# Four places for the values, other places for the results, and side work in other slots, in a fused attention and gated MLP kernel

## The chip, the cores and the metric

The kernel runs on one core of a Trainium2 chip. The core has five engines with their own instruction queues: TensorE (PE in the rows, with PEld for its weight loads), VectorE (DVE), ScalarE (ACT), GpSimd (POOL) and SyncE (SP, which here only issues DMAs). Each engine works through its own list in order and waits on semaphores. The metric is the device time of one execution in microseconds; before the change it was 2021.7 us, the median of three runs (2020.38 to 2023.5).

## The reference, cut to what matters

Four sequences of 3008 tokens go through an attention without softmax, and all 12032 tokens then go through a gated MLP. Everything is float32.

```python
scores = (z @ z.T) / S                  # per batch, z is S x 64
attn = np.maximum(scores, 0.0) ** 2
x = u * (attn @ v)                      # u, v: 4 x 3008 x 256
gate = 1 / (1 + np.exp(-(x @ w_gate)))  # 256 -> 1536
val = x @ w_val
out = (gate * val) @ w_out              # 1536 -> 256
```

## The kernel before, in words

**Float32 from two halves.** Operands of matmuls are split in a rounded high part and a low rest (`x_high` and `x_low`, `h_high` and `h_low`, and so on), and a product is three matmuls: high by high, high by low, low by high.

**Stage 1, attention.** `steps` is a list of 288 steps: 4 batches of 72, in each of them 6 chunks of 512 queries, in each of these 12 pairs of key blocks. In a step PE computes scores two steps ahead and then the product with v. ACT takes scale, relu and square and rounds the result (`ah`, line 367); DVE takes the rest (`al`, line 372). Scores are symmetric, so later chunks load stored, turned blocks back (`r<-shared`, line 461) in place of computing them. Work that isn't part of a step is hung on step numbers in the tables `before` and `after`: loads of the next batch, the eighteen `Narrow` jobs that turn the weights from float64 words into halves and store them in DRAM (line 726 ff.), and, in the last twelve steps, the making of the first group's x. The attention's sums go to the DRAM tensor `sums`.

**Stage 2, the MLP.** Tokens go in 12 groups of 1024 (two tiles t of 512; the last group 2 of 384), and a group takes six rounds J, one for each 256 columns of the hidden width. In a round the 2 x 2 blocks of x by weights are made with seven products in place of eight (Winograd's form of Strassen's scheme), once for the gate and once for the value: P1, P6, P2, P7, P5, P4, P3, each three matmuls into one of PSUM's banks 0 to 3, which are taken in turn. `copy_s1` (ACT) and seven `join`s (DVE, line 641) add the products up to four blocks, named 11, 21, 12 and 22. Gate blocks lie in `g_t` (four places in the area `spare`), value blocks in `y_t` (area `keep`). `gate` is ACT's sigmoid, `gated` (POOL, line 649) multiplies value by gate, `h_high` (ACT, line 653) and `h_low` (POOL, line 658) split the result. Its product with `w_out`, eight outs of three matmuls (lines 674 to 676), runs one round later: after the second, fourth, fifth and last product of gate and of value, `beside` puts one out. So the order on PE in a round is, for the gate and again for the value: P1 P6 out P2 P7 out P5 out P4 P3 out, 66 matmuls in all.

**Slots.** `beside(J, slot)` also runs what the table `extra` holds for that slot; slots 0 to 3 lie in the gate's half, 4 to 7 in the value's. Slots 0 and 4 stand after the join of P6, 1 and 5 after that of P7, 2 and 6 after those of P5, 3 and 7 after the last join of the half, that of P3. On DVE such side work stands between these joins. It is what the next group needs: `load_sums`, `load_u` (8 DMAs of 64 KB for one tile t), `turn_u` (a transpose of u), `make_x` (u times sums), `sum_x` (T1 to T4, four differences), and four times `x_high` and `x_low`. `finish` transposes a finished result out of PSUM and sends it out with four DMAs.

**What sets the order.** The order is written by hand; nothing is scheduled anew. An instruction waits until its inputs are there and until earlier readers of the place that it writes are done. Before the change the four value blocks share two places: 11 and 21 have one, 22 and 12 the other. A join that writes 12 thus waits for the `gated` that reads 22.

The places that the change touches, for following it in the code:

```python
t = part(keep_a, 4 * (C % 2), 2 * CH)                      # line 504, keep
y_t = {c: part(keep_a, 2 * x, CH) for c, x in ((11, 0), (22, 1), (21, 0), (12, 1))}   # line 625
osb = t_p[:, 2 + h] if t else part(keep_a, 4 + 2 * h, CH)  # line 681, finish
```

## Time and profile before

| what | value |
|---|---|
| median of three runs | 2021.7 us |
| the profiled execution | 2018.66 us |
| its span in the trace | 2016.2 us |
| PE busy | 1918.4 us, 95% |
| DVE busy | 1505.0 us, 75% |
| ACT busy | 1151.9 us, 57% |
| POOL busy | 781.3 us, 39% |
| granted TensorE clock | 0.999 of full speed (2.4 GHz) |

The page cuts the span in 40 slices. PE stands at 9 tenths or more in all of them but two, at 8. POOL is at three tenths in the first slice, at zero up to the eighteenth and at five to seven tenths in the rest: stage 2 begins at about 895 us. A matmul's record is longer than the step from one matmul to the next, since matmuls are pipelined; PE's progress is read from starts, and its losses from the waits that the trace puts down to another engine. The profiled execution is 3.0 us under the median of the runs.

### The profile page before, as it was taken

To read this page: it belongs to the slowest core of one execution; us is meant where nothing else is said; L and a number is where in the kernel's file an instruction comes from. 1 tells how busy PE (TensorE), PEld (TensorE's weight loads), DVE (VectorE), ACT (ScalarE), POOL (GpSimd) and SP (SyncE) were. 2 spreads that over 40 slices of the span, in tenths; PEclk is the share of its full clock that TensorE was granted. 3 is DMA by queue.
4 is the path that set the end of the run, shared out by engine and by line. 5 is a ranking of instruction groups with operands and counts; after the bars stand their busy time and mean duration, and the time that the engine had idled before them with its cause. 6 is when DMAs were issued, how large, how long until landed. Compare 5 with 4: busy or idle time off the path is not lost.

```text
span 2016.2 us, 26100 instructions
## 1 busy us (share of the span) xinstructions
PE 1918.4 (95%) x8870; PEld 1649.7 (82%) x8870; DVE 1505.0 (75%) x1946; ACT 1151.9 (57%) x1504; POOL 781.3 (39%) x609
## 2 busy tenths in 40 slices
PE   9999999999999999999989999999999999999998
PEld 7887988798887988887878777777777777778787
DVE  7688788787887776567776867676767777777765
ACT  8886888768886787644434434343434343434443
POOL 3000000000000000007766767676767666767675
PEclk9999999999999999999999999999999999999999
DMA  6689689996899797776324251414152423333231
GB/s 139 142 236 255 193 197 240 259 287 153 227 267 248 219 237 184 195 187 213 92 81 108 66 120 71 118 55 118 56 132 70 107 86 87 93 98 80 83 95 34
DMA packets 596725, 298.76 MB, mean 148 GB/s; under 512 B 529904, under 2 KB 547056, under 8 KB 596592
## 3 DMA queue, kind: packets, MB, share of 16 engines
q1 hardware_dynamic: 591312, 294.48, 55.4%
q0 software_dynamic: 1024, 2.10, 0.5%
q8 instruction: 69, 1.13, 0.2%
q10 hardware_dynamic: 4256, 0.52, 0.2%
q14 instruction: 64, 0.52, 0.1%
HBM read 189.92 MB, written 101.06 MB: 144 GB/s over the span
## 4 chain that ended last, share of the span: by engine, by line
PE 40%; POOL 27%; issue 18%; SPq 4%; ACT 4%; DVE 3%; DMA 3%; DVEq 0%; POOLq 0%; ACTq 0%
POOL spare L649 13%; PE banks L494 9%; PE banks L487 9%; PE banks L489 8%; POOL h L658 8%; POOL v L658 4%; PE banks L344 3%; PE banks L343 3%; POOL al L658 2%; PE banks L616 2%; ACT h L653 2%; PE banks L618 2%; PE banks L617 2%; DMA r<-shared 1%; PE banks L675 1%
## 5 line engine op out<-in xcount | busy, mean ns | idle before, releaser
L649 POOL TENSOR_TENSOR spare<-keep,spare 128x512 f32<-128x512 f32 (+1 forms) x284 | 360.3, 1279 | 1139.6 <-DMA turned<-in_u_dram 854.3
L372 DVE TENSOR_TENSOR al<-r,ah 128x1024 fp32r<-128x1024 f32 (+1 forms) x287 | 341.3, 1191 | 179.0 <-ACT ah L367 173.9
L487 PE MATMUL banks<-ah,v 128*128 128x512 f32 (+1 forms) x1152 | 429.6, 376 | 5.2 <-ACT ah L367 4.8
L489 PE MATMUL banks<-ah,v 128*128 128x512 f32 (+1 forms) x1104 | 414.2, 375 | 0.0
L494 PE MATMUL banks<-al,v 128*128 128x512 f32 (+1 forms) x1152 | 341.1, 378 | 10.9 <-DVE al L372 9.5
L367 ACT ACTIVATE ah<-r 128x1024 fp32r<-128x1024 f32 (+1 forms) x251 | 255.4, 1034 | 51.6 <-DMA r<-shared 15.6
L645 ACT ACTIVATE spare<-spare 128x512 f32<-128x512 f32 (+1 forms) x288 | 177.8, 619 | 166.4 <-DVE spare L641 166.2
L494 PEld LDWEIGHTS banks<-al,v 128*128 128x128 f32 x1152 | 215.6, 189 | 46.2 <-DVE al L372 21.3
L487 PEld LDWEIGHTS banks<-ah,v 128*128 128x128 f32 x1152 | 218.3, 189 | 34.3 <-ACT ah L367 8.1
L653 ACT ACTIVATE h<-spare 128x512 fp32r<-128x512 f32 (+1 forms) x144 | 89.6, 622 | 271.0 <-POOL spare L649 268.6
L658 POOL TENSOR_TENSOR h<-spare,h 128x512 fp32r<-128x512 f32 (+1 forms) x144 | 213.1, 1480 | 55.9 <-ACT h L653 55.9
L641 DVE TENSOR_TENSOR zt<-banks,zt 128x512 f32<-128x512 f32 (+1 forms) x288 | 193.2, 671 | 52.8 <-ACT zt L635 45.4
L489 PEld LDWEIGHTS banks<-ah,v 128*128 128x128 f32 x1104 | 209.2, 189 | 24.4
L351 ACT ACTIVATE r<-banks 128x1024 f32<-128x1024 f32 (+2 forms) x173 | 167.2, 967 | 99.3 <-PE banks L344 97.6
L641 DVE TENSOR_TENSOR spare<-banks,zt 128x512 f32<-128x512 f32 (+1 forms) x288 | 187.0, 669 | 31.9 <-POOL v L658 21.8
L641 DVE TENSOR_TENSOR keep<-banks,zt 128x512 f32<-128x512 f32 (+1 forms) x144 | 97.1, 674 | 117.6 <-POOL spare L649 111.8
L352 ACT ACTIVATE r<-r 128x1024 f32<-128x1024 f32 (+2 forms) x173 | 174.3, 1008 | 5.5
L616 PE MATMUL banks<-z,v 128*128 128x512 f32 x378 | 146.9, 389 | 21.2 <-DVE keep L641 9.8
L653 ACT ACTIVATE v<-spare 128x512 fp32r<-128x512 f32 (+1 forms) x144 | 89.4, 621 | 117.5 <-POOL spare L649 114.8
L618 PE MATMUL banks<-z,v 128*128 128x512 f32 x378 | 143.3, 379 | 0.0
L635 ACT ACTIVATE zt<-banks 128x512 f32<-128x512 f32 (+1 forms) x144 | 83.2, 577 | 91.1 <-PE banks L618 77.6
L343 PE MATMUL banks<-zq,z 128*128 128x512 f32 (+2 forms) x348 | 126.7, 367 | 1.4 <-DVE zq L775 1.4
(150 smaller groups left out, 3828.8 us busy)
## 6 DMA issues: line engine op xcount, KB each, us to landing
v<-w_gv SPq DMA_DIRECT2D x75, 896.0 KB, 4.7
r<-shared SPq DMA_DIRECT2D x72, 512.0 KB, 4.7
shared<-turned SPq DMA_DIRECT2D x236, 128.0 KB, 2.9
r<-shared SPq DMA_DIRECT2D x38, 448.0 KB, 5.0
shared<-spare SPq DMA_DIRECT2D x128, 128.0 KB, 3.3
turned<-sums SPq DMA_DIRECT2D x22, 512.0 KB, 5.9
turned<-in_u_dram SPq DMA_DIRECT2D x176, 64.0 KB, 2.5
w_gv<-w SPq DMA_DIRECT2D x24, 448.0 KB, 4.2
```

Of the source, the lines that this page charges most:

```text
L343: nc.tensor.matmul(sc[:, j, 0 : n - q0], h, q, start=True, stop=False)
L367: nc.scalar.activation(ah[:, :, 0:n], r[:, :, 0:n], AF.Copy)
L372: nc.vector.tensor_tensor(al[:, :, 0:n], r[:, :, 0:n], f32(ah[:, :, 0:n]), op=ALU.subtract)
L487: nc.tensor.matmul(o, vh[:, j, ds], moving(ah[:, j, 0:n]), start=(k == 0 and j == 0), stop=False)
L489: nc.tensor.matmul(o, vl[:, j, ds], moving(ah[:, j, 0:n]), start=False, stop=False)
L494: nc.tensor.matmul(acc[:, d, 0:n], vh[:, j, ds], moving(al[:, j, 0:n]), start=False, stop=stop)
L616: nc.tensor.matmul(o, wt[:, 0, w], xh, start=True, stop=False)
L618: nc.tensor.matmul(o, wt[:, 1, w], xh, start=False, stop=True)
L641: nc.vector.tensor_tensor(to[:, 0:m], bank(J, value, name), s_t[other][:, 0:m], op=ALU.add)
L649: (nc.vector if J == last else nc.gpsimd).tensor_tensor(g, y, g, op=ALU.mult)
L653: nc.scalar.activation(h_of(c)[0][:, 0:m], g_t[c][:, 0:m], AF.Copy)
L658: nc.gpsimd.tensor_tensor(lo[:, 0:m], g_t[c][:, 0:m], f32(hi[:, 0:m]), op=ALU.subtract)
```

## The change

It does these things:

- `y_t` has four places, in all of `keep_a`. `gated` writes its product into the value's place and not the gate's, and `h_high` and `h_low` read it there; the gate's place is free once `gated` has run.
- `finish` puts all four results in the area of x's sums `t_p` (the upper half of `turned_a`), none in `keep_a`.
- `load_u` for the first tile of the next group moves from slot 0 of the group's first round to slot 3 of the second, behind the DMAs of `finish` on SP's queue; `turn_u`, `make_x`, `sum_x`, `x_high`, `x_low` of the next group get other slots.
- The first group's sums, u and x are loaded, turned and multiplied at steps 226 to 247 (early in the last batch) and not in the last twelve, in areas that are free there (`raw_a`, `zt_a`, half of `keep_a`); the sums and splits of it stay in the last twelve steps.
- The eighteen `Narrow` jobs start at other steps: two and not five in the first batch, seven in the second and the third, two early in the last. Three of the five weight loads of the last batch are put later.

```diff
@@ keep
-        t = part(keep_a, 4 * (C % 2), 2 * CH).rearrange("p (h q) -> p h q", h=NB)
+        if C == B * NCH - 1:
+            t = part(turned_a, 8, 2 * CH)
+        else:
+            t = part(keep_a, 4 * (C % 2) if b < B - 1 else 0, 2 * CH)
+        t = t.rearrange("p (h q) -> p h q", h=NB)
...
+    def x_of(G):
+
+        return part(turned_a if G else raw_a, 0, 8 * KB).rearrange("p (t h q) -> p t h q", t=2, h=NB)
+
+    def u_of(G):
+
+        places = (t_p[:, 0:2], t_p[:, 2:4]) if G else (part(zt_a, 0, 2 * CH), part(keep_a, 4, 2 * CH))
+        return places if G else [ap.rearrange("p (i q) -> p i q", i=2) for ap in places]
...
-    y_t = {c: part(keep_a, 2 * x, CH) for c, x in ((11, 0), (22, 1), (21, 0), (12, 1))}
+    y_t = {c: part(keep_a, 2 * x, CH) for x, c in enumerate((11, 21, 12, 22))}
...
-        (nc.vector if J == last else nc.gpsimd).tensor_tensor(g, y, g, op=ALU.mult)
+        (nc.vector if J == last else nc.gpsimd).tensor_tensor(y, y, g, op=ALU.mult)
...
-        nc.scalar.activation(h_of(c)[0][:, 0:m], g_t[c][:, 0:m], AF.Copy)
+        nc.scalar.activation(h_of(c)[0][:, 0:m], y_t[c][:, 0:m], AF.Copy)
...
-        nc.gpsimd.tensor_tensor(lo[:, 0:m], g_t[c][:, 0:m], f32(hi[:, 0:m]), op=ALU.subtract)
+        nc.gpsimd.tensor_tensor(lo[:, 0:m], y_t[c][:, 0:m], f32(hi[:, 0:m]), op=ALU.subtract)
...
-        osb = t_p[:, 2 + h] if t else part(keep_a, 4 + 2 * h, CH)
+        osb = t_p[:, 2 * t + h]
...
-        starts = [*range(24, 54, 7), *range(84, 127, 7), *range(156, 199, 7)][: 3 * NF]
+        starts = [24, 31, *range(84, 127, 7), *range(156, 199, 7), 221, 228]
...
+        g = 3 * per
+        at(after, g + 2, load_w, 0, 1)
+        at(after, g + 6, load_w, 1, 1)
+        for t in range(2):
+            at(after, g + 10 + t, load_sums, 0, t)
+        for t in range(2):
+            at(after, g + 14 + 10 * t, load_u, 0, t)
+            at(before, g + 20 + 10 * t, turn_u, 0, t)
+            at(before, g + 21 + 10 * t, make_x, 0, t)
+        for J in range(3):
+            at(after, g + 28 + 5 * J, load_w, J, 0)
...
-                at(extra, (J, 0), load_u, G, 0)
-                    (1, 3, turn_u, 0), (1, 3, load_u, 1), (1, 6, make_x, 0), (2, 3, turn_u, 1), (2, 6, make_x, 1),
+                    (1, 3, load_u, 0), (1, 7, turn_u, 0), (1, 7, load_u, 1), (2, 3, make_x, 0), (2, 7, turn_u, 1),
...
```

On DVE, in the second round of a group (L641 is the join before, L652 the same line in the change; `banks` are PSUM, `zt`, `spare` and `keep` hold partial sums, gate blocks and value blocks; L552 and L565 are `turn_u`). Before:

```order
L641 TENSOR_TENSOR spare<-banks,spare 128x512
L641 TENSOR_TENSOR spare<-banks,zt 128x512
L552 STREAM_TRANSPOSE turned<-turned 128x1024
L641 TENSOR_TENSOR zt<-banks,zt 128x512
L641 TENSOR_TENSOR keep<-banks,zt 128x512
```

In the change:

```order
L652 TENSOR_TENSOR spare<-banks,spare 128x512
L652 TENSOR_TENSOR spare<-banks,zt 128x512
L652 TENSOR_TENSOR zt<-banks,zt 128x512
L652 TENSOR_TENSOR keep<-banks,zt 128x512
L652 TENSOR_TENSOR spare<-banks,zt 128x512
L652 TENSOR_TENSOR keep<-banks,spare 128x512
L652 TENSOR_TENSOR zt<-banks,zt 128x512
L652 TENSOR_TENSOR keep<-banks,spare 128x512
L652 TENSOR_TENSOR keep<-banks,zt 128x512
L565 STREAM_TRANSPOSE turned<-turned 128x1024
L652 TENSOR_TENSOR zt<-banks,zt 128x512
```

The transpose of u stood after the gate's last join; it stands seven joins later, after the value's last join.

On SP, from the sums' load of one group to the next weight loads (L544 and L556 are `load_u`, L685 and L696 the DMAs of `finish`, L593 and L604 `load_w`). Before:

```order
L533 DMA turned<-sums 128x2x512 x2
L544 DMA turned<-in_u_dram 32x16x32 x8
L685 DMA out_dram<-keep 32x16x32 x8
L685 DMA out_dram<-turned 32x16x32 x4
L593 DMA v<-w_gv 128x1792
L685 DMA out_dram<-turned 32x16x32 x4
L544 DMA turned<-in_u_dram 32x16x32 x8
L593 DMA v<-w_gv 128x1792 x5
```

In the change:

```order
L545 DMA turned<-sums 128x2x512 x2
L696 DMA out_dram<-turned 32x16x32 x12
L604 DMA v<-w_gv 128x1792
L696 DMA out_dram<-turned 32x16x32 x4
L556 DMA turned<-in_u_dram 32x16x32 x16
L604 DMA v<-w_gv 128x1792 x5
```

The first eight loads of u moved from ahead of the sixteen result DMAs to behind them.

On DVE, in the fourth to sixth round of a group (L581 and L592 are `x_low`, L572 and L583 `sum_x`, here of an odd to even group, whose operands lie in `z` and `zq`). Before:

```order
L572 TENSOR_TENSOR turned<-turned 128x512
L641 TENSOR_TENSOR spare<-banks,zt 128x512 x2
L641 TENSOR_TENSOR spare<-banks,spare 128x512
L641 TENSOR_TENSOR zt<-banks,zt 128x512
L572 TENSOR_TENSOR turned<-turned 128x512
L641 TENSOR_TENSOR spare<-banks,spare 128x512
L641 TENSOR_TENSOR spare<-banks,zt 128x512
L581 TENSOR_TENSOR z<-turned,z 128x1024
L641 TENSOR_TENSOR zt<-banks,zt 128x512
L572 TENSOR_TENSOR turned<-turned 128x512
L641 TENSOR_TENSOR keep<-banks,zt 128x512
```

In the change:

```order
L592 TENSOR_TENSOR z<-turned,z 128x1024
L652 TENSOR_TENSOR zt<-banks,zt 128x512
L583 TENSOR_TENSOR turned<-turned 128x512
L652 TENSOR_TENSOR spare<-banks,zt 128x512 x2
L583 TENSOR_TENSOR turned<-turned 128x512
L652 TENSOR_TENSOR spare<-banks,spare 128x512
L652 TENSOR_TENSOR zt<-banks,zt 128x512
L652 TENSOR_TENSOR spare<-banks,spare 128x512
L652 TENSOR_TENSOR spare<-banks,zt 128x512
L583 TENSOR_TENSOR turned<-turned 128x512
L652 TENSOR_TENSOR zt<-banks,zt 128x512
```

The first split now stands ahead of the differences, at the end of a round's value half, and the differences go in slots 0, 1, 3 and 4.

## Rows read from the trace of the kernel before

**Rows 1.** Waits from 905 to 1920: engine, line, releaser: us, times, longest.
```profile
DVE keep L641 <- POOL spare L649: 100.9, 61, 1.8
DVE turned L552 <- DMA out_dram<-turned: 38.3, 9, 5.3
PE banks L616 <- DVE keep L641: 23.5, 42, 0.6
PE banks L675 <- POOL h L658: 19.9, 32, 1.1
...
PE banks L616 <- DVE zt L641: 16.8, 10, 2.8
...
PE banks L616 <- DVE spare L641: 5.3, 20, 0.3
...
PE banks L675 <- POOL al L658: 3.0, 10, 0.3
```
**Rows 2.** PE, same place in two following groups: start, us, line, [idle before, releaser].
```profile
1204.21 0.48 PE L616 MATMUL banks<-x,v 128*128 128x512 f32 x1 [1.49 <-DVE zt L641]
...
1299.24 0.48 PE L616 MATMUL banks<-z,v 128*128 128x512 f32 x1 [1.54 <-DVE zt L641]
```
**Rows 3.** PE, the value's P1 in two following rounds that have no wait.
```profile
1358.88 0.38 PE L616 MATMUL banks<-z,v 128*128 128x512 f32 x1
1373.13 0.38 PE L616 MATMUL banks<-v 128*128 128x512 f32 x1
```
**Rows 4.** Timeline of all engines at the end of such a round.
```profile
1366.01 0.38 PE L616 MATMUL banks<-v,wgv 128*128 128x512 f32 x1
...
1366.19 2.53 POOL L649 TENSOR_TENSOR spare<-keep,spare 128x512 f32<-128x512 f32 x2
...
1366.90 0.60 ACT L635 ACTIVATE zt<-banks 128x512 f32<-128x512 f32 x1 [2.02 <-PE banks L618]
...
1367.51 0.69 DVE L641 TENSOR_TENSOR keep<-banks,zt 128x512 f32<-128x512 f32 x1 [1.83 <-POOL spare L649]
```
**Rows 5.** DVE in a group's second round: the transpose of u.
```profile
1297.36 1.25 DVE L552 STREAM_TRANSPOSE turned<-turned 128x1024 f32<-128x1024 f32 x1 [3.98 <-DMA out_dram<-turned]
```
**Rows 6.** SP's queue: the last result DMAs of that group change.
```profile
1290.40 2.20 SPq L685 DMA_DIRECT2D out_dram<-turned  x4
```
**Rows 7.** SP's queue: the second eight loads of u in the first group.
```profile
918.18 11.78 SPq L544 DMA_DIRECT2D turned<-in_u_dram  x8
```
**Rows 8.** DMA issues: KB each, median us from issue to landing.
```profile
turned<-in_u_dram SPq DMA_DIRECT2D x176, 64.0 KB, 2.5
```
**Rows 9.** Timeline, side work of DVE beside POOL: `make_x`, then `sum_x`.
```profile
1301.69 1.22 DVE L562 TENSOR_TENSOR turned<-turned 128x1024 f32<-128x1024 f32 x1
1301.88 2.15 POOL L658 TENSOR_TENSOR h<-spare,h 128x512 fp32r<-128x512 f32 x1 [0.74 <-ACT h L653]
...
1321.39 1.28 POOL L658 TENSOR_TENSOR al<-spare,v 128x512 fp32r<-128x512 f32 x1
...
1321.66 1.55 DVE L572 TENSOR_TENSOR turned<-turned 128x512 f32<-128x512 f32 x1
1322.62 1.74 POOL L649 TENSOR_TENSOR spare<-keep,spare 128x512 f32<-128x512 f32 x1
```
**Rows 10.** End of stage 1: DVE's transpose of u for the first group.
```profile
882.64 1.25 DVE L552 STREAM_TRANSPOSE turned<-turned 128x1024 f32<-128x1024 f32 x1 [4.60 <-DMA turned<-in_u_dram]
```
**Rows 11.** PE's waits from 800 to 910 us.
```profile
PE banks L494 <- DVE al L372: 3.6, 1, 3.6
PE banks L617 <- DVE z L581: 1.2, 1, 1.2
```
**Rows 12.** PE's waits from 120 to 190 us, in steps of moved jobs.
```profile
PE banks L494 <- DVE al L372: 2.8, 6, 0.9
PE banks L487 <- ACT ah L367: 1.5, 2, 0.8
```
**Rows 13.** Window: us; busy PE, PEld, DVE, ACT, POOL; clock; DMA share; GB/s.
```profile
703.00:740.00 37.00, 37.00 (x175) 32.74 (x174) 27.10 (x24) 30.16 (x31) 0.00 (x0) 1.00 0.98 234
```

More of the change, by code (lines that the diff above doesn't have):

```diff
@@ L512 @@
     groups = [(t0, min(CH, (N - t0) // 2)) for t0 in range(0, N, 2 * CH)]
-    x_p = part(turned_a, 0, 8 * KB).rearrange("p (t h q) -> p t h q", t=2, h=NB)
     t_p = part(turned_a, 8, 8 * KB).rearrange("p (i q) -> p i q", i=4)
@@ L525, in operand, with source @@
         return [part(a, o, 2 * CH, F32R).rearrange("p (i q) -> p i q", i=2) for a, o in places]
-    def source(i):
-        return x_p[:, i] if i < 2 else t_p[:, 2 * (i - 2) : 2 * (i - 2) + 2]
+    def x_of(G):
[3 more added lines that the diff above has]
+        return places if G else [ap.rearrange("p (i q) -> p i q", i=2) for ap in places]
+    def source(G, i):
+        return x_of(G)[:, i] if i < 2 else t_p[:, 2 * (i - 2) : 2 * (i - 2) + 2]
     def load_sums(G, t):
@@ L532, in load_sums @@
         t0 += t * n
-        nc.sync.dma_start(x_p[:, t, :, 0:n], sums[:, :, t0 : t0 + n])
+        nc.sync.dma_start(x_of(G)[:, t, :, 0:n], sums[:, :, t0 : t0 + n])
     u_rows = u.rearrange("b s d -> (b s) d")
@@ L539, in load_u @@
         t0 += t * n
-        raw = t_p[:, 0:2].rearrange("p h (T d) -> p h T d", d=32)
+        raw = u_of(G)[0].rearrange("p h (T d) -> p h T d", d=32)
         for g in range(4):
@@ L550, in turn_u @@
         n = groups[G][1]
+        raw, ut = u_of(G)
         if n == CH:
-            nc.vector.transpose(
-                out=t_p[:, 2:4].rearrange("p i q -> p (i q)"), in_=t_p[:, 0:2].rearrange("p i q -> p (i q)")
-            )
+            nc.vector.transpose(out=ut.rearrange("p i q -> p (i q)"), in_=raw.rearrange("p i q -> p (i q)"))
         else:
             for h in range(NB):
-                nc.vector.transpose(out=t_p[:, 2 + h, 0:n], in_=t_p[:, h, 0:n])
+                nc.vector.transpose(out=ut[:, h, 0:n], in_=raw[:, h, 0:n])
     def make_x(G, t):
         n = groups[G][1]
-        x = x_p[:, t, :, 0:n]
-        nc.vector.tensor_tensor(x, x, t_p[:, 2:4, 0:n], op=ALU.mult)
+        x = x_of(G)[:, t, :, 0:n]
+        nc.vector.tensor_tensor(x, x, u_of(G)[1][:, :, 0:n], op=ALU.mult)
     def sum_x(G, i):
         n = groups[G][1]
-        x = x_p[:, :, :, 0:n]
+        x = x_of(G)[:, :, :, 0:n]
         t = t_p[:, :, 0:n]
@@ L575, in x_high @@
         n = groups[G][1]
-        nc.scalar.activation(operand(G, i)[0][:, :, 0:n], source(i)[:, :, 0:n], AF.Copy)
+        nc.scalar.activation(operand(G, i)[0][:, :, 0:n], source(G, i)[:, :, 0:n], AF.Copy)
     def x_low(G, i):
@@ L580, in x_low @@
         hi, lo = (ap[:, :, 0:n] for ap in operand(G, i))
-        nc.vector.tensor_tensor(lo, source(i)[:, :, 0:n], f32(hi), op=ALU.subtract)
+        nc.vector.tensor_tensor(lo, source(G, i)[:, :, 0:n], f32(hi), op=ALU.subtract)
     def w_place(J, value):
@@ L731 @@
                 at(after if name == "store" else before, g + x, getattr(job, name))
-        g = len(steps) - NPAIR
-        for t in range(2):
-            at(after, g, load_sums, 0, t)
-        at(after, g, load_u, 0, 0)
-        for x, (J, value) in enumerate(((0, 0), (0, 1), (1, 0), (1, 1), (2, 0))):
-            at(after, 3 * per + 4 * x, load_w, J, value)
-        at(before, g + 2, turn_u, 0, 0)
-        at(after, g + 2, load_u, 0, 1)
-        at(before, g + 3, make_x, 0, 0)
-        at(before, g + 4, turn_u, 0, 1)
-        at(before, g + 5, make_x, 0, 1)
+        g = 3 * per
[9 more added lines that the diff above has]
+            at(after, g + 28 + 5 * J, load_w, J, 0)
+        g = len(steps) - NPAIR
         for i in (T1, T3):
-            at(before, g + 6, sum_x, 0, i)
+            at(before, g + 2, sum_x, 0, i)
         for i in (T2, T4):
-            at(before, g + 7, sum_x, 0, i)
-        for x, i in ((6, B1), (7, B2), (8, T12), (9, T34)):
+            at(before, g + 3, sum_x, 0, i)
+        for x, i in ((4, B1), (5, B2), (6, T12), (8, T34)):
             at(before, g + x, x_high, 0, i)
@@ L857 @@
                     at(extra, (J, 0), load_sums, G, t)
-                at(extra, (J, 0), load_u, G, 0)
                 line = (
-                    (1, 3, turn_u, 0), (1, 3, load_u, 1), (1, 6, make_x, 0), (2, 3, turn_u, 1), (2, 6, make_x, 1),
-                    (3, 0, sum_x, T1), (3, 1, x_high, B1), (3, 2, sum_x, T3), (3, 3, x_low, B1),
-                    (3, 4, sum_x, T2), (3, 5, x_high, B2), (3, 6, sum_x, T4), (3, 7, x_low, B2),
-                    (4, 0, x_high, T12), (4, 2, x_low, T12), (4, 4, x_high, T34), (4, 6, x_low, T34),
+                    (1, 3, load_u, 0), (1, 7, turn_u, 0), (1, 7, load_u, 1), (2, 3, make_x, 0), (2, 7, turn_u, 1),
+                    (3, 3, make_x, 1), (3, 4, x_high, B1), (3, 7, x_low, B1),
+                    (4, 0, sum_x, T1), (4, 1, sum_x, T3), (4, 3, sum_x, T2), (4, 4, sum_x, T4),
+                    (4, 5, x_high, T12), (4, 7, x_low, T12), (5, 0, x_high, T34), (5, 1, x_low, T34),
+                    (5, 2, x_high, B2), (5, 3, x_low, B2),
                 )
```

## The prediction

> **What bounds the kernel now.** I read the waits first, then the timeline of PE, then those of the engines that PE waits for. PE is busy in nearly every slice, so only time in which PE stands still can be won, and the reader should first see how much that is. Stage 2 is a repetition. In a pair of rounds without a wait, the same product starts 1373.13 - 1358.88 = 14.25 us apart [rows 3]: 66 matmuls of 0.216 us, three of them 0.65 us. Six rounds without a wait would be 85.5 us. The same place in two following groups lies 1299.24 - 1204.21 = 95.0 us apart [rows 2]. So a group loses 9.5 us, and 10.7 groups (the last is smaller) lose 101 us.
>
> The waits say to whom [rows 1]. PE's five rows add up to 23.5 + 19.9 + 16.8 + 5.3 + 3.0 = 68.5 us in 114 waits. The other 32.5 us of the 101 are what stands around a wait (the matmul behind it starts late too): 0.285 us for each. With that, the rows are worth: value joins (`keep`) 23.5 + 12.0 = 35.5; gate joins (`spare`) 5.3 + 5.7 = 11.0; `zt` joins 16.8 + 2.9 = 19.7; POOL's `h_low` (`h` and `al`) 22.9 + 12.0 = 34.9 us.
>
> Behind the value joins stands a place. In [rows 4] POOL runs two `gated` from 1366.19 to 1368.72, and DVE's join of 12 stands from 1365.68 to 1367.51: 1.83 us, until the first of them (that of 22) has read the place which 12 shares. DVE waits so 61 times, 100.9 us in all, and 42 waits of PE follow. Behind the `zt` joins stands the transpose of u: it waits 3.98 us for result DMAs that still read its place [rows 5], in nine groups 38.3 us [rows 1], and every join behind it is late, then `gated`, then `h_low` (1.1 us, the longest wait on POOL).
>
> **Four places for values.** Nothing is added: the same POOL, ACT and DVE instructions, of the same shapes, at other addresses. What goes is the wait of 1.8 us. A value place is now free after `h_low` of the round before. The last of these follows the two `gated` of [rows 4] by four more operations of 1.26 us, and so ends at 1373.8; the next join of 12 can come at 1365.68 + 14.25 = 1379.9, 6 us later. A gate place is free after `gated`, one to three POOL operations earlier than now. What is late next is PE itself: a join can start 0.89 us after its product's first matmul (1366.01 and 1366.90, [rows 4]). A bank is taken again four products later; for the join of P6 that is seven places of 0.65 us, less 0.89 and less the 0.7 us of a join, so DVE may be 3.0 us late before PE feels it. I take both rows, 35.5 + 11.0 = 46.5 us, as gone. Bounds: 0, if POOL's queue is late in any case, and 46.5.
>
> **u behind the results.** The transpose could have started at 1297.36 - 3.98 = 1293.4 [rows 5]. Its new place is half a round later, 1300.5. Its result place is free then (1297.36 + 0). But its loads are now issued behind the results: the last four result DMAs leave SP at 1292.6 after 2.2 us of issue [rows 6]; eight loads take twice that, 4.4 us, and land 2.5 us after [rows 8]: 1299.5 if nothing holds them. If they move only once the results have landed, 1297.4 + 4.4 + 2.5 = 1304.3. The transpose waits 0 to 3.8 us; I take 2. Queued behind it on DVE is the P6 join of the next round, which has 3.0 us to spare. So the 19.7 us go, at no cost. Only in the first group is it different: there the weights of five rounds and `w_out` stand on the queue, the eight loads at this place took 11.8 us of issue [rows 7], and I add 3 us for one long wait.
>
> **Side work in other slots.** Per group DVE has two `make_x`, four `sum_x`, four `x_low`. They are there before and after; what counts is what they meet. Behind the last join of a half (slots 3 and 7) DVE's next product ends three places later, 1.94 us, less a join 1.25; a `make_x` takes 1.2. So DVE is on time again. POOL isn't free of them: `make_x` at 1301.69 and `h_low` at 1301.88 end one after the other, 2.15 us for POOL where 1.28 is usual, and `sum_x` at 1321.66 takes 1.55 us, since it begins only when POOL's operation ends at 1322.67, and the next one of POOL takes 1.74 [rows 9]. So they exclude each other, by turns. In slot 3 POOL has run its burst (from the value's first `gated` to the next round's last `h_low`, eight operations of 1.26 us, 10.1 of 14.25 us). In slot 7 it is in the middle of it. I walk through the fourth to the sixth round: `x_low` in slot 7 of the fourth pushes the second half of the burst by its 1.2 us, and `h_low` of 22 (now 1368.72 + 1.26 = 1370.0 in [rows 4]) has 0.8 us to spare before PE's second matmul of out 22, seven places and a matmul after 1366.01, some more if the joins ahead of it are on time; the first difference in the fifth's slot 0 pushes it by 0.6 more: PE waits 0.6. In the sixth `x_low` in slots 7 and 1 do the same: PE waits some 0.8. That is 1.5 us and two times 0.285, 2.1 us a group, 22 us in all, in place of the 34.9 us on POOL: a gain of 13. Bounds: 35 (none of these waits is left) to -20 (each of the four `x_low` makes PE wait its whole 1.2 us, 51 us with the surroundings).
>
> Two transposes of u now stand in slot 7 too. In the rows they fall in POOL's pauses, so what they do to a running POOL operation isn't shown. Bounds: 0, or like the `x_low` 2 x 1.2 us a group less what POOL has to spare, some 0.3 us, 3 us in all. I take 0. The Trainium skill (SBUF — State Buffer, Who interferes with whom) says that a VectorE operation with two inputs in SBUF excludes a GpSimd operation that reads SBUF, and that one with a single input outside the fast modes doesn't contend; by it the transposes cost 0, and no run here shows it yet.
>
> **End of stage 1.** The first group's transpose waited 4.60 us for its DMA in the last twelve steps, and PE stood 3.6 us for the `al` behind it on DVE, then 1.2 for a late `x_low` [rows 10, 11]. Loads, transposes and `make_x` move some fifty steps ahead; `al` is then on time and four splits remain. Gain 3.6 + 1.2 + 2 x 0.285 = 5.4 us. Their new place has two transposes and two `make_x`, 4.9 us of DVE in twenty steps; DVE is busy 27.1 of 37 us there, and PE without a gap [rows 13]. The cover is that slack, and six steps between load and transpose. DMA share is 0.98 there, and 16 small loads, two loads of sums and two jobs come to it while three weight loads leave: cost 0 to 5 us, I take 0.
>
> **Jobs.** Three of five jobs leave the first batch. PE waited 4.3 us in 8 waits in their steps, with surroundings 6.6 us [rows 12]. Bounds: 6.6, all of it, to -6.6, if the jobs bring as much where they go; I take +3, since stage 1 is full of DMA at the ends of all batches.
>
> **Sum.** 46.5 + 19.7 - 3 + 13 + 5.4 + 3 = 84.6 us. From the profiled execution's 2018.66 us that leaves 1934.1; the median of the runs lies 3.0 higher, so 1937. I predict 1936 us.
>
> **Rivals.**
> POOL takes over: the places remove DVE's wait, but POOL's burst, pushed by side work, becomes what PE waits for. For it: [rows 9]; against it: 10 of 14.25 us, so POOL has 4 us a round. Then POOL costs 51 to 55 us in place of 35, and the gain is 84.6 - 13 - 20 = 52: 1970 us.
>
> Everything goes: PE never waits in stage 2, and the jobs' stalls go. 101 + 5.4 + 6.6 = 113 us: 1909. Against it is the exclusion in [rows 9].
>
> The transpose waits for u again, now at slot 7. For it: the loads stand behind sixteen results, and in the first group they took 11.8 + 2.5 = 14.3 us. Slot 7 is 7.1 us behind slot 3, so the wait would be 7.2 us, 4.2 beyond what DVE has to spare, 10.7 x 4.2 = 45 us: 1981. The same mechanism ends on the other side, slower than before, from 18 us on from slot 3 to the last landing: 84.6 / 10.7 = 7.9 us a group are then lost beyond the 3.0 us; at 20 us it is 10 us a group, 2043 us. Against it: results landed within 5 us of their issue [rows 5, 6].
>
> The change doesn't do what it says: the value joins still wait on POOL, as their places are now held to `h_low`. Then 46.5 is 0 and the time is 1983. Against it: the 6 us above.
>
> **How the numbers follow.** Forecast 0.64; POOL takes over 0.13; everything goes 0.08; u late but faster 0.07, u late and slower 0.04; the places give nothing 0.04, half of it with u late too and no change left. The forecast's own range is 1920 to 1955: the terms for side work (13, from 0 to 25) and stage 1. From 1909 to 1981 the cases hold more than 8 in 10; I give 1908 to 1976. Within 0.2% (4 us, about what a measurement here can tell from none) I see 0.02; faster 0.94; slower 0.04.
>
> **What would show it.** In the profile after: no row of value joins on `gated` (100.9 us now); a group 85.5 + 2 = 87.6 us; transposes of u with a wait under 3 us; PE's remaining waits in stage 2 on POOL's `h_low` of 22 in a group's fifth and sixth round; no wait of 3.6 us at the end of stage 1. Wrong, if a group stays above 91 us, if PE's waits on POOL grow over 35 us, or if new waits on DMA stand in the last batch.

## The result, and the profile after

The changed kernel took 1937.9 us (median of 4 runs, 1936.4 to 1939.0) where the kernel before took 2022.6 beside it (2020.4 to 2025.9). The ratio is 0.9579, with a 95% interval of 0.9563 to 0.9596: 84.7 us won. The prediction was 1936, with a sum of 84.6 us. The total is right. The experiments show that its largest terms are not.

The page of the changed kernel (profiled execution 1938.98 us): first line, busy times, and the share of each engine in the chain of work that ended last. In the kernel before this chain lay on PE for 40% and on POOL for 27% of the span.

```profile
span 1937.2 us, 26164 instructions
...
PE 1895.7 (98%) x8870; PEld 1659.7 (86%) x8870; DVE 1514.5 (78%) x1946; ACT 1151.5 (59%) x1504; POOL 765.4 (40%) x609
...
PE 77%; POOL 5%; DVE 4%; issue 4%; DMA 3%; ACT 3%; SPq 3%; DVEq 0%; ACTq 0%; POOLq 0%
```

The span is 79 us shorter, and the time in which PE does nothing falls from 97.8 us (2016.2 less 1918.4) to 41.5. The rest of the 79, 22.7 us, is PE's busy time. Most likely it is matmuls behind a wait, whose records are longer: the surroundings that the prediction priced apart.

Waits of the changed kernel from 905 to 1920 us, first those of DVE, then all of PE (engine, line, releaser: us, times, longest). They answer to [rows 1].

```profile
DVE zt L652 <- ACT zt L646: 64.3, 80, 1.5
DVE keep L652 <- PE banks L629: 45.2, 85, 0.6
...
DVE turned L565 <- DMA turned<-in_u_dram: 20.4, 10, 8.8
...
PE banks L627 <- DVE zt L652: 7.9, 11, 5.7
PE banks L686 <- POOL al L669: 7.5, 10, 0.8
```

The value joins no longer wait for POOL (100.9 us before): their largest wait is now PE's own product. PE's waits fall from 68.5 us in 114 to 15.4 us in 21. Priced as in the prediction this is 53.1 + 93 x 0.285 = 79.6 us. Stage 2, from its first product to its last matmul, measures 78.3 us less: 1038.8 us (892.1 to 1930.9) for 1117.1 (892.75 to 2009.9).

PE in the changed kernel (start, us, line, [idle before, releaser]): a wait of stage 1, the first group, and the waits of the repetition. They answer to [rows 2].

```profile
753.77 0.48 PE L487 MATMUL banks<-ah,v 128*128 128x512 f32 x1 [2.75 <-ACT ah L367]
...
930.94 0.79 PE L627 MATMUL banks<-z,wgv 128*128 128x512 f32 x1 [5.66 <-DVE zt L652]
...
1064.58 0.48 PE L686 MATMUL banks<-al,al 128*128 128x512 f32 x1 [0.81 <-POOL al L669]
...
1151.89 0.48 PE L686 MATMUL banks<-al,al 128*128 128x512 f32 x1 [0.80 <-POOL al L669]
...
1155.41 0.48 PE L627 MATMUL banks<-z,v 128*128 128x512 f32 x1 [0.22 <-DVE zt L652]
```

The same place in two following groups lies 1151.89 - 1064.58 = 87.31 us apart (95.0 before, 87.6 predicted, 85.5 without any wait). What is left per group is 0.8 us on `h_low` of 22 (its low half lies in `al`) and 0.2 us three microseconds later. The 5.66 us stand once, in the first group; the 2.75 us are new.

The other engines of the changed kernel around those places, SP, ACT, DVE and POOL. They answer to [rows 5, 7, 9].

```profile
737.16 5.75 SPq L556 DMA_DIRECT2D zt<-in_u_dram  x8
743.01 4.53 SPq L398 DMA_DIRECT2D shared<-turned  x8
747.63 0.57 SPq L461 DMA_DIRECT2D r<-shared  x1
...
752.66 1.06 ACT L367 ACTIVATE ah<-r 128x1024 fp32r<-128x1024 f32 x1 [6.53 <-DMA r<-shared]
...
929.07 1.25 DVE L565 STREAM_TRANSPOSE turned<-turned 128x1024 f32<-128x1024 f32 x1 [8.83 <-DMA turned<-in_u_dram]
...
1104.17 1.25 DVE L565 STREAM_TRANSPOSE turned<-turned 128x1024 f32<-128x1024 f32 x1 [0.72 <-DMA turned<-in_u_dram]
...
1117.11 2.52 POOL L660 TENSOR_TENSOR keep<-keep,spare 128x512 f32<-128x512 f32 x2
1117.62 1.23 DVE L565 STREAM_TRANSPOSE turned<-turned 128x1024 f32<-128x1024 f32 x1
...
1131.34 3.49 POOL L660 TENSOR_TENSOR keep<-keep,spare 128x512 f32<-128x512 f32 x2
1131.87 1.84 DVE L592 TENSOR_TENSOR v<-turned,v 128x1024 fp32r<-128x1024 f32 x1
```

The transpose of u waits 0.72 us here, (20.4 - 8.83) / 9 = 1.3 us on average after the first group, for loads and not for result DMAs. By the prediction DVE may be 3.0 us late there, and no wait of PE follows at that place. In the first group it waits 8.83 us. At 1131 a split meets two `gated`: POOL takes 3.49 us for 2.52, DVE 1.84 us for 1.21.

In stage 1 the wait of 3.6 us [rows 11] is gone. But ACT stands 6.53 us for a stored block that SP could not issue before 747.63, behind eight loads of the first x and eight stores, and PE stands 2.75 us behind ACT. In the two profiles stage 1 ends 0.7 us earlier in all (892.1 for 892.75).

### The profile page after: what moved, and what is told of

Same layout as the page of the kernel before. It is cut to its first block, busy times and chain, and to the rows that moved or that the text cites. A ratio compares the mean times of both kernels' runs of the same rounds, so it can differ in the third digit from the quotient of the medians.

```text
span 1937.2 us, 26164 instructions
## 1 busy us (share of the span) xinstructions
PE 1895.7 (98%) x8870; PEld 1659.7 (86%) x8870; DVE 1514.5 (78%) x1946; ACT 1151.5 (59%) x1504; POOL 765.4 (40%) x609
## 3 DMA queue, kind: packets, MB, share of 16 engines
q8 instruction: 69, 1.13, 0.2%
## 4 chain that ended last, share of the span: by engine, by line
PE 77%; POOL 5%; DVE 4%; issue 4%; DMA 3%; ACT 3%; SPq 3%; DVEq 0%; ACTq 0%; POOLq 0%
PE banks L494 10%; PE banks L487 9%; PE banks L627 9%; PE banks L489 9%; PE banks L629 9%; PE banks L628 9%; PE banks L686 5%; PE banks L687 5%; PE banks L685 5%; POOL keep L660 3%; PE banks L344 3%; PE banks L343 3%; DMA r<-shared 2%; DVE al L372 1%; ACT ah L367 1%
## 5 line engine op out<-in xcount | busy, mean ns | idle before, releaser
L660 POOL TENSOR_TENSOR keep<-keep,spare 128x512 f32<-128x512 f32 (+1 forms) x284 | 377.1, 1339 | 1069.2 <-DVE keep L652 1069.2
L652 DVE TENSOR_TENSOR zt<-banks,zt 128x512 f32<-128x512 f32 (+1 forms) x288 | 193.4, 672 | 71.7 <-ACT zt L646 66.8
L664 ACT ACTIVATE h<-keep 128x512 fp32r<-128x512 f32 (+1 forms) x144 | 89.7, 623 | 256.2 <-POOL keep L660 252.8
L669 POOL TENSOR_TENSOR h<-keep,h 128x512 fp32r<-128x512 f32 (+1 forms) x144 | 196.9, 1368 | 56.8 <-ACT h L664 56.8
L652 DVE TENSOR_TENSOR spare<-banks,zt 128x512 f32<-128x512 f32 (+1 forms) x288 | 188.1, 673 | 19.4 <-PE banks L629 18.4
L664 ACT ACTIVATE v<-keep 128x512 fp32r<-128x512 f32 (+1 forms) x144 | 89.1, 619 | 71.6 <-POOL keep L660 69.5
L343 PE MATMUL banks<-zq,z 128*128 128x512 f32 (+2 forms) x348 | 126.9, 367 | 1.4 <-DVE zq L787 1.4
L344 PE MATMUL banks<-zq,z 128*128 128x512 f32 (+2 forms) x348 | 126.8, 367 | 0.0
```

The source lines that it names most:

```text
L343: nc.tensor.matmul(sc[:, j, 0 : n - q0], h, q, start=True, stop=False)
L344: nc.tensor.matmul(sc[:, j, 0 : n - q0], l, q, start=False, stop=True)
L652: nc.vector.tensor_tensor(to[:, 0:m], bank(J, value, name), s_t[other][:, 0:m], op=ALU.add)
L660: (nc.vector if J == last else nc.gpsimd).tensor_tensor(y, y, g, op=ALU.mult)
L669: nc.gpsimd.tensor_tensor(lo[:, 0:m], y_t[c][:, 0:m], f32(hi[:, 0:m]), op=ALU.subtract)
```

## The experiments

### The parts of stage 2 taken apart

**Splits and differences alone.** The kernel before, with only this row of its slot table changed:

```diff
-  (3, 0, sum_x, T1), (3, 1, x_high, B1), (3, 2, sum_x, T3), (3, 3, x_low, B1),
-  (3, 4, sum_x, T2), (3, 5, x_high, B2), (3, 6, sum_x, T4), (3, 7, x_low, B2),
-  (4, 0, x_high, T12), (4, 2, x_low, T12), (4, 4, x_high, T34), (4, 6, x_low, T34),
+  (3, 4, x_high, B1), (3, 7, x_low, B1),
+  (4, 0, sum_x, T1), (4, 1, sum_x, T3), (4, 3, sum_x, T2), (4, 4, sum_x, T4),
+  (4, 5, x_high, T12), (4, 7, x_low, T12), (5, 0, x_high, T34), (5, 1, x_low, T34),
+  (5, 2, x_high, B2), (5, 3, x_low, B2),
```

> The kernel before with the new slots of splits and differences alone; the two transposes of u and make_x stay at slots 3 and 6 of the second and third round, and all else as before. The new slots together took 61 us in the run before this. Theory of the prediction's rows (the transposes' wait for result DMAs is worth 19.7 us, which come back): 1960 + 20 = 1980 us. Rival (the wait of 4 us on DVE also holds up value joins and POOL, so it is worth more than the zt row, 30 us or more): 1990 us or more. Second rival (it is worth little, since other waits cover it): 1965 us.

2019.6 us (10 runs), ratio 0.9980 [0.9971, 0.9989]: 3 us won. Its waits from 905 to 1920:

```profile
DVE turned L552 <- DMA out_dram<-turned: 37.9, 9, 4.8
...
PE banks L616 <- DVE zt L641: 35.9, 31, 2.7
PE banks L616 <- DVE keep L641: 16.3, 41, 0.6
PE banks L675 <- POOL h L658: 6.5, 6, 1.1
PE banks L675 <- POOL al L658: 3.0, 10, 0.3
```

These are all of PE's rows. Beside [rows 1], POOL's `h` row loses 13.4 us, `keep` 7 and `spare` all of its 5.3, but the `zt` row gains 19. A row that shrinks is not a gain until the sum of the rows shrinks. Even the sum misleads here: 6.8 us and 26 waits less would be 14 us by the prediction's price, and 3 were won. The gain of the `zt` row is a second wait in each group, 1.32 us at 1346.30, beside the one behind the transpose (1.77 us at 1303.14).

**The transpose's wait kept, make_x moved too.** As the next experiment, from which the edit is shown, but the first transpose of u (and the second load of u behind it) stays where it waits for result DMAs:

```diff
-  (1, 7, turn_u, 0), (1, 7, load_u, 1), (2, 3, make_x, 0), (2, 7, turn_u, 1),
+  (1, 3, turn_u, 0), (1, 3, load_u, 1), (2, 3, make_x, 0), (2, 7, turn_u, 1),
```

> The kernel before with the new slots (1960 us as a whole), but the first transpose of u at slot 3 of the second round, where it waits about 4 us for the result DMAs; make_x, the second transpose, splits and differences stay at their new slots. Theory (one wait of 4 us for a DMA is the root of the rows of zt, of POOL's h and of the value joins behind it, 4.5 us of PE's waits a group): most of the 58 us that the two transposes and make_x brought together go again, and the time is 2000 to 2010 us. Rival (make_x in slot 6, in the middle of POOL's burst, is what costs): 1965 us, and the wait of 4 us on DVE stays without PE waiting.

1998.3 us, ratio 0.9880 [0.9867, 0.9894]. Its waits, same stretch:

```profile
DVE turned L552 <- DMA out_dram<-turned: 37.8, 9, 5.6
...
PE banks L616 <- DVE zt L641: 35.4, 31, 3.4
PE banks L616 <- DVE keep L641: 13.0, 31, 0.8
...
PE banks L675 <- POOL h L658: 2.2, 9, 0.3
```

That is 21 us less than with splits and differences alone, from `make_x` and the second transpose in their new slots. POOL's `h` row falls to 2.2 us although the first transpose waits as before; the `zt` row stays.

**All new slots, nothing else.** The kernel before with the new table; the first load of u, the places and stage 1 stay.

```diff
-  (1, 3, turn_u, 0), (1, 3, load_u, 1), (1, 6, make_x, 0), (2, 3, turn_u, 1), (2, 6, make_x, 1),
...
+  (1, 7, turn_u, 0), (1, 7, load_u, 1), (2, 3, make_x, 0), (2, 7, turn_u, 1),
+  (3, 3, make_x, 1), (3, 4, x_high, B1), (3, 7, x_low, B1),
...
```

> The kernel before with the new slots of the side work alone (turn_u at slot 7 of the second and third round and all behind it; u's first loads stay at slot 0 of the first round, the two value places, the results' places and all of stage 1 as before). Theory of the prediction: the long wait of the transposes goes (19.7 us) and PE's waits on POOL shrink (13 us), while the value and gate joins still make PE wait, so about 2022 - 33 = 1989 us. Rival (the slots do most of it, the places only matter when DVE is late already): 2022 - 75 = 1947 us or less a few.

1960.3 us, ratio 0.9692 [0.9669, 0.9715]: 62 of the 85 us, with value places as before. Its waits, same stretch:

```profile
DVE keep L641 <- POOL spare L649: 106.1, 68, 2.1
...
PE banks L616 <- DVE zt L641: 15.3, 21, 1.2
PE banks L616 <- DVE keep L641: 7.6, 22, 0.8
PE banks L675 <- POOL al L658: 3.0, 10, 0.3
```

DVE waits for a place as long as ever, 106.1 us, and PE's rows fall from 68.5 to 26 us. So two thirds of the value joins' row on PE, the gate joins' row and POOL's `h` row had come from the side work in its old slots and not from the places alone. The step from the experiment before this, 38 us, is the first transpose's (with the load behind it): 4.2 us a group in nine groups, for a wait of 4.2 us.

These are PE's waits behind one late transpose in the experiment before this:

```profile
1292.42 0.48 PE L616 MATMUL banks<-z,v 128*128 128x512 f32 x1 [1.67 <-DVE zt L641]
...
1296.38 0.48 PE L675 MATMUL banks<-h,ah 128*128 128x512 f32 x1 [0.25 <-POOL h L658]
...
1298.34 0.48 PE L616 MATMUL banks<-z,wgv 128*128 128x512 f32 x1 [0.60 <-DVE keep L641]
```

They add up to 2.5 us, 3.4 with the prediction's price for the surroundings. With all new slots none of them is left, and the first wait of the group, 1.23 us on a `zt` join (at 1319.79), stands three rounds later. In the kernel before the same place had 1.54 us [rows 2] and then 1.12 on `h`, 0.61 and 0.43 on `keep` (1304.08, 1306.04, 1320.98). What the transpose's slot is worth with `make_x` in its old one was not tried.

**The places undone.** The changed kernel with two places for values, products written to the gate's place:

```diff
-    y_t = {c: part(keep_a, 2 * x, CH) for x, c in enumerate((11, 21, 12, 22))}
+    y_t = {c: part(keep_a, 2 * x, CH) for c, x in ((11, 0), (22, 1), (21, 0), (12, 1))}
...
-        (nc.vector if J == last else nc.gpsimd).tensor_tensor(y, y, g, op=ALU.mult)
+        (nc.vector if J == last else nc.gpsimd).tensor_tensor(g, y, g, op=ALU.mult)
...
```

> The changed kernel with the four places alone undone: 11 and 21 share a value place, 22 and 12 the other, and gated writes into the gate's place again. Theory of the prediction (the places are worth their rows, 46.5 us): DVE's join of 12 waits 1.8 us for the gated of 22 in most rounds, PE's waits on value and gate joins come back with some 40 us, and the time is about 1938 + 46 = 1984 us. Rival (side work is now out of the way, so that DVE's 3.0 us to spare cover the wait of 1.8): DVE waits 100 us on POOL as before, but PE hardly does, and the time is 1940 to 1950 us.

1959.7 us, ratio 0.9697 [0.9676, 0.9718]: 22 us slower than the changed kernel, where the prediction's 46.5 us would give 1984. Its waits, same stretch:

```profile
DVE keep L652 <- POOL spare L660: 107.3, 68, 2.1
...
PE banks L627 <- DVE zt L652: 19.7, 22, 4.3
PE banks L627 <- DVE keep L652: 7.5, 22, 0.8
```

What comes back is the wait of 1.3 us a group on a `zt` join (1319.20) and smaller ones behind it. The time comes within 1 us of the kernel with all new slots and nothing else. So the rest of the change (u's loads behind the results, stage 1, the jobs) comes to nothing in sum: in the two profiles stage 1 is 5 us shorter here and stage 2, with the long wait of the first group, 5 us longer.

**A place of its own for 12, old slots.** The kernel before, all side work where it was. There is room for three value places only, and gate places stay held until `h_low`; the low half of 21 moves next to that of 22, so `al` names both here.

```diff
-    y_t = {c: part(keep_a, 2 * x, CH) for c, x in ((11, 0), (22, 1), (21, 0), (12, 1))}
+    y_t = {c: part(keep_a, 2 * x, CH) for c, x in ((11, 0), (22, 1), (21, 0), (12, 2))}
...
-        osb = t_p[:, 2 + h] if t else part(keep_a, 4 + 2 * h, CH)
+        osb = t_p[:, 2 + h] if t else part(raw2_a, 0, CH) if h else part(keep_a, 6, CH)
...
```

> The kernel before, with a value place of its own for block 12 (three places: 11 and 21 share one, 22 and 12 no longer do), and with every piece of side work at its old slot; so the transpose of u still waits its 4 us for result DMAs. The results of the first tile go to one value place and to 2 KB that were part of the `raw` area, and the attention's last sums to the upper half of `turned_a`. Theory (the rows of the place waits and those of the transpose's wait price one loss twice; the places alone are worth no more than the 22 us that they are worth on top of the new slots): DVE's wait of its value joins for POOL, 101 us, falls under 15 us, and PE wins 10 to 22 us of it: 2000 to 2012 us, 2005 likeliest; the 4-us wait and PE's row of `zt` joins stay or grow. Rival (what an edit wins depends on which comes first, and the rows price it rightly where it comes first): the value joins' 35.5 us go, 1987 us, at most 1992.

2014.7 us (10 runs), ratio 0.9968 [0.9958, 0.9978]: 7 us won beside its own runs of the kernel before (2021.4), less than even my theory had. Its waits, same stretch:

```profile
DVE spare L641 <- POOL al L658: 55.8, 60, 1.8
...
DVE spare L641 <- POOL v L658: 35.6, 64, 0.6
DVE turned L552 <- DMA out_dram<-turned: 34.3, 9, 4.8
...
PE banks L675 <- POOL al L658: 24.1, 42, 1.3
PE banks L675 <- POOL h L658: 18.5, 30, 1.1
```

The row of value joins on POOL is gone, on DVE and on PE. In its place the joins of the next gate wait for `h_low`, which reads the gate place: 55.8 + 35.6 = 91.4 us, where such waits were 36.3 in the kernel before (19.5 on `v` and 16.8 on `h`). PE's own waits on POOL go from 22.9 to 42.6 us. One such place in the timeline:

```profile
1226.64 1.27 POOL L658 TENSOR_TENSOR al<-spare,v 128x512 fp32r<-128x512 f32 x1
...
1227.94 0.69 DVE L641 TENSOR_TENSOR spare<-banks,spare 128x512 f32<-128x512 f32 x1 [1.22 <-POOL al L658]
...
1227.96 0.48 PE L675 MATMUL banks<-al,ah 128*128 128x512 f32 x1 [0.66 <-POOL al L658]
```

DVE and PE wait for the same POOL operation, and now at the same time. With old slots the rival "POOL takes over" is what happens. The other half of the change, a gate place free after `gated`, was not tried by itself, nor four value places in the old slots.

### What the changed kernel still loses

**Side work in POOL's pauses.** The changed kernel with the splits and differences in slots where POOL stands:

```diff
-  (3, 3, make_x, 1), (3, 4, x_high, B1), (3, 7, x_low, B1),
-  (4, 0, sum_x, T1), (4, 1, sum_x, T3), (4, 3, sum_x, T2), (4, 4, sum_x, T4),
-  (4, 5, x_high, T12), (4, 7, x_low, T12), (5, 0, x_high, T34), (5, 1, x_low, T34),
-  (5, 2, x_high, B2), (5, 3, x_low, B2),
+  (2, 5, x_high, B1), (3, 3, make_x, 1), (3, 4, x_low, B1),
+  (4, 3, sum_x, T1), (4, 3, sum_x, T3), (4, 4, sum_x, T2), (4, 5, sum_x, T4),
+  (4, 6, x_high, T12), (5, 3, x_low, T12), (5, 2, x_high, T34), (5, 4, x_low, T34),
+  (5, 6, x_high, B2), (5, 7, x_low, B2),
```

> The changed kernel with another table: the splits and differences that take two inputs in SBUF stand in POOL's pauses (x_low of B1 in the fourth round's slot 4, T12 and T34 in the sixth's 3 and 4, B2 in its slot 7, T1 and T3 in the fifth's slot 3, T2 in 4, T4 in 5), so none is in the fourth's or the fifth's slot 7 or in slots 0 and 1. Theory (POOL and DVE exclude each other, and what is left of PE's waits on POOL, 0.8 us a group and 0.2 us on a join behind it, is POOL's burst pushed by side work): these waits go, 10.7 x 1.9 = 20 us with what stands around them, 1918 us, a group 85.5 us. Rival (the burst is late by itself, POOL's own eight operations and the waits for ACT set it): the 0.8 us stay, 1936 to 1940 us.

1922.5 us, ratio 0.9507 [0.9487, 0.9527]. PE's waits from 905 to 1920:

```profile
PE banks L627 <- DVE zt L652: 4.1, 1, 4.1
PE banks L686 <- POOL al L669: 1.2, 4, 0.4
PE banks L686 <- POOL h L669: 0.8, 1, 0.8
```

Both repeated waits of the changed kernel are gone, 15 us with their surroundings. So POOL's burst is not late by itself: side work of DVE pushed it. Two `gated` ahead of the wait at 1151.89 took POOL 3.50 us in the changed kernel (at 1147.12), and the same two take 2.53 here (at 1142.04), which agrees with the exclusion by turns in the prediction's walk through the rounds.

**The first group's u early.** Attention's last sums go to the upper part of `t_p`, so that the first load of u can stand a round earlier, ahead of the weights.

```diff
-            t = part(turned_a, 8, 2 * CH)
+            t = part(turned_a, 12, 2 * CH)
...
-  (1, 3, load_u, 0),
+  (0 if G == 1 else 1, 0 if G == 1 else 3, load_u, 0),
```

> The changed kernel, with u's loads for the second group back at slot 0 of the first round, ahead of the weights (the attention's last sums go through the other half of the place so that it is free). Theory: PE's one wait of 5.66 us at 931 us is DVE's transpose that waits 8.83 us for these loads behind 7 MB of weights; it goes, and the time falls by 5 to 6 us to 1932 us. Rival: the loads were late for another reason (the results' place or the sums' store), and nothing changes.

1931.9 us, ratio 0.9551 [0.9530, 0.9573]; its runs (1927.1 to 1933.4) lie under all runs of the changed kernel. PE's row of `zt` joins is now "2.3, 10, 0.2" for "7.9, 11, 5.7": the one long wait is gone, and it cost some 6 us where I had taken 3. The intervals of the two ratios touch, so the 6 is rough; in the profiles of four other kernels with these loads where the change has them the wait is 3.6 to 4.1 us.

**Loads of u one slot later in the repetition.**

```diff
-  (1, 3, load_u, 0),
+  (1, 5, load_u, 0),
```

> The changed kernel with u's first loads of a group at slot 5 in place of slot 3 of the second round, some 4 us later; the transpose stays at slot 7. Theory (DVE has 3.0 us to spare there): its wait grows from 1.2 to some 4 to 5 us, PE waits 1 to 2 us a group on a zt join and perhaps again on POOL behind it, and the time is 1955 to 1970 us. Rival (the loads leave SP when the results have landed, whatever the slot): the wait and the time stay, 1938 us.

1936.6 us, ratio 0.9574 [0.9561, 0.9587], not to be told from the changed kernel; my theory of 1955 to 1970 us was wrong and the rival right. SP's queue in it:

```profile
1002.93 2.32 SPq L696 DMA_DIRECT2D out_dram<-turned  x4
1005.29 13.46 SPq L556 DMA_DIRECT2D turned<-in_u_dram  x16
```

SP works through its list in order: the loads start right behind the results here (1005.29) as in the changed kernel (1008.75, the results ending at 1008.70), and the transpose waits 1.4 us on average after the first group, for 1.3.

**First x late again.** The changed kernel with load, transpose and product of the first x in the last twelve steps, as before.

```diff
-        g = 3 * per
...
+        g = len(steps) - NPAIR
...
-            at(after, g + 14 + 10 * t, load_u, 0, t)
-            at(before, g + 20 + 10 * t, turn_u, 0, t)
-            at(before, g + 21 + 10 * t, make_x, 0, t)
...
+        at(after, g, load_u, 0, 0)
...
+        at(before, g + 2, turn_u, 0, 0)
...
```

> The changed kernel with the first group's sums, u, transposes and x back in the last twelve steps. Theory: the wait of 3.6 us at the end of stage 1 and those behind it come back (5.4 us) and the wait of 2.75 us at 754 us goes, since u's sixteen loads stand no more ahead of r's loads on SP: 1938 + 5.4 - 3 = 1940 us. Rival (the wait at 754 us has nothing to do with u's loads): it stays and the time is 1943 us.

1939.4 us, ratio 0.9587 [0.9574, 0.9600]: 1.5 us more, within what the runs scatter. A wait of 4.1 us at the end is back, and that of 2.75 us at 754 us is gone. In these profiles early x wins the one and pays the other.

**Jobs at their old steps.**

```diff
-        starts = [24, 31, *range(84, 127, 7), *range(156, 199, 7), 221, 228]
+        starts = [*range(24, 54, 7), *range(84, 127, 7), *range(156, 199, 7)][: 3 * NF]
```

> The changed kernel with the weight jobs at their steps before (five in the first batch, none in the last). Theory of the prediction (moving them is worth 3 us in the first batch): PE's waits from 120 to 190 us go back from 2.1 to 4.3 us, the wait of 2.75 us at 754 us stays, and the time is 1938 + 3 = 1941 us. Rival (two jobs in the last batch, with their stores ahead of r's loads on SP, are the cause of the wait at 754 us): that wait goes and the time is 1937 us or less.

1932.7 us, ratio 0.9558 [0.9543, 0.9573]: 5 us less than the changed kernel, where the prediction had 3 us more. PE's waits from 100 to 890 us are 6.7 + 6.7 us here and 9.3 + 4.0 there: equal in sum. That of 754 us is gone and those of the first batch are back, so the rows of single profiles don't carry these 5 us. Nor do the stages: in the two profiles stage 1, the only one that the edit touches, ends 1.3 us earlier here (890.8 for 892.1), and stage 2, the same in both, is 4.3 us shorter. The intervals of the two ratios overlap. So the 3 us are not there; that moving the jobs cost 5 us is not shown.

**All three together, with x between the two.** Pauses, the first u early, and the first x at steps 250 to 270.

```diff
...
-            at(after, g + 14 + 10 * t, load_u, 0, t)
...
+            at(after, g + 38 + 8 * t, load_u, 0, t)
...
```

> The changed kernel with the splits in POOL's pauses, u's loads of the second group ahead of the weights, and the first group's sums, u, transposes and x at steps 250 to 270 in place of 226 to 247. Theory: 1922.5 us of the run with the pauses, less 6 us for the first group's one wait, less 3 us for the wait at 754 us: 1914 us. Rival (loads of u bring the same wait of ACT on r's loads wherever they stand in the last batch): 1917 us.

1911.0 us, ratio 0.9446 [0.9432, 0.9460], faster than both kernels. It is 26.9 us under the changed kernel. The pauses (15.4) and the first u (5.9) alone gave 21.3; the other 5.6 us go with x's new steps, which were not tried alone. In stage 2 (905 to 1920 us) PE has four waits left, 1.8 us:

```profile
PE banks L686 <- POOL al L669: 1.0, 3, 0.4
PE banks L686 <- POOL h L669: 0.8, 1, 0.8
```

**The same with the jobs at their old steps.** The edit is that of the jobs above.

> The kernel of the combined run (1911 us) with the weight jobs at their steps before. Theory (the jobs cost 5 us by standing ahead of r's loads early in the last batch, and that is gone in the combined run only for u's loads): 1908 us. Rival (with u's loads out of the way the jobs in the last batch cost nothing and spare the first batch 2 to 3 us of waits): 1913 us.

1912.4 us, ratio 0.9457 [0.9444, 0.9470]: no difference. With x later, the jobs' new steps cost nothing. The wait at 754 us needs both the jobs and x's loads in these steps: it stands, at 1.1 to 3.0 us, in all five profiles that have both, and is 0.4 us or none where the jobs (old steps), x's loads (first x late) or both have gone.

## Why the prediction was right in its sum and wrong in its terms

In the order of its steps, predicted and measured:

| step | predicted us | measured us | by |
|---|---|---|---|
| four places | +46.5 | +22 in the new slots; +7 for three places in the old ones | places undone; three places |
| u behind the results | +19.7 | +38 (first transpose) | slots alone, early transpose |
| first group's wait | -3 | -6 | first u early |
| side work in other slots | +13 | +24 (splits and differences 3, `make_x` and second transpose 21) | early transpose, splits alone |
| end of stage 1 | +5.4 | +1.5, within the scatter | first x late |
| jobs | +3 | -5, not clear of the scatter | jobs at old steps |

The three large terms sum to 79 and to 84. The measured ones are steps of one chain from the kernel before to the changed one, so that they sum to nearly the whole is no proof of each. In another order they are others: the places come last in this chain with 22 us, and three places put first gave 7.

**The step that failed** is "the rows are worth": each row of PE's waits was given to the releaser that it names, with 0.285 us for the surroundings of each wait. The total so found is good (79.6 us by that price, 78.3 measured in stage 2). The division is not. A wait row names only the last thing waited for, and a delay moves from row to row with whatever else is late. While two value places stayed, PE's row of value joins fell from 23.5 us by 16.3 and 13.0 to 7.6 (kernel before, splits alone, early transpose, all new slots), the gate joins' 5.3 went with the first step, and POOL's `h` went from 19.9 by 6.5 and 2.2 to nothing. I had booked the first two rows to the places alone. The `zt` row, which I had booked to the transpose alone, rose from 16.8 to 35.9 while the transpose stayed as it was, since splits and differences in their new slots brought a `zt` wait of their own; that one, 15.3 us, was left when the transpose's had gone, and the places remove most of it. The price of 0.285 us for the surroundings is no constant either: by the time of stage 2 beside that of the combined kernel it is 0.28 us a wait with all new slots and 0.42 with the splits alone.

**Places.** "The wait of 1.8 us goes" came true. What it is worth depended on the rest: 7 us with three places in the old slots, where POOL is next; 22 with all that the change does, in the new ones. The sentence "what is late next is PE itself" holds in the new slots only; in the old ones gate joins were next, since a gate place stayed taken until `h_low`.

**u behind the results.** That the transpose stops waiting for results, that its loads land in time (1.3 us on average for the 2 I took) and that DVE's 3.0 us hide it was right. Only its price, the `zt` row alone, was half of the 38 us that it gives. The issue of the first eight loads, priced at 4.4 us, takes 6.4 in the group at 1096 us (last section).

**Side work beside POOL.** What remains is of the size given, but not all of it where it was given: one wait of 0.8 us a group on `h_low` of 22, in the sixth round, and 0.2 us on a join behind it, where the walk had 0.6 us in the fifth round and 0.8 in the sixth. The group takes 87.31 us for 87.6, and placing the work in POOL's pauses removes the waits. But the 13 us were half of the 24 that these slots gave: with `make_x` moved, PE's waits of 1.13 us on `h` and 0.43 on a value join, in the group at 1300 us, fell to 0.25 and nothing, and the second I had booked to the places.

**Transposes beside POOL.** I took 0: at 1117.62 the transpose takes 1.23 us, and the two POOL operations around it 2.52, as long as alone. The rule of the Trainium skill (SBUF — State Buffer, Who interferes with whom) on operations with one input agrees.

**Stage 1.** The 3.6-us wait left as said, but DVE's slack was the wrong cover to look at: the cost came on SP's queue, where sixteen small loads and stores delayed one load that ACT needed. My bound of 5 us for that was right and my 0 was not. The two terms together, 8.4 us, were too large. The first product of stage 2 starts at 892.8 to 897.4 us in four profiles with stage 1 as before and at 889.4 to 893.3 in five with that of the change: 3.4 us earlier on average, with ranges that overlap. How this divides between x and the jobs stays open.

The range held since the sum was tied to PE's whole loss (9.5 us a group) and to what would remain of it (2 us a group), and errors in dividing it cancel. Both ends were right: the combined kernel, with almost no wait, takes 1015.5 us for stage 2, 101.6 less than the kernel before, for the 101 us given. That the sum came within 1 us is luck: the interval of the ratio alone is 82 to 88 us, stage 2 won 2 us more than its terms (78.3 for 76.2), and stage 1 less than its 8.4.

## What to carry to other kernels

Price a repetition by its total loss and by an estimate of what will remain; the row of a releaser is no price of a cause. Before a row is booked to a cause, look whether its waits follow an earlier, longer wait in the same repetition, and count them to that one. A wait on an engine that is off the bound (101 us on DVE) can be removed for 7 us if the engine behind it is late as well. What a fix is worth depends on which others are in place, so undo one at a time, and in more than one order.

## What was not expected of the hardware

Loads of u occupy SP mostly for as long as stores of results do, 0.49 us each, but single ones for much longer. The sixteen loads in one group of the changed kernel, in two halves (shortest, median and longest in ns, first and last start):

```profile
L556 SPq DMA_DIRECT2D turned<-in_u_dram x8: 486/487/2652, 1096.0 to 1101.9; - x8
...
L556 SPq DMA_DIRECT2D turned<-in_u_dram x8: 312/487/488, 1105.4 to 1109.0; - x8
```

The first half, right behind the results, takes 6.4 us since one load stands 2.65 us; the prediction had 4.4 from the price of stores. In the first group of the kernel before, with weight loads in flight, eight took 11.78 us [rows 7]. The row of 13.46 us for sixteen loads (1005.29, above) is not issue alone: between the halves SP waits for the first transpose, which reads the place that the second half writes. Why single loads stand is not shown.

DVE's split beside POOL's products lost time on both sides (1.84 us for 1.21, 3.49 for 2.52), which a busy time of 40% on POOL doesn't show.
